# Second batch's fills and sums of squares rearranged, and three late output tiles stored by halves, in a fused cosine attention and GELU feed-forward kernel

## The chip, the cores and the metric

The kernel runs on one core of one Trainium2 chip. The metric is the device time of one execution in microseconds (us); the time of a kernel is the median of several runs.

## The reference

The input is q, k and v of shape 8 x 12 x 448 x 64 (batch, heads, sequence, head dimension), fp32, and two weight matrices. What is computed, cut to what matters:

```python
q_n = q / (norm(q, axis=-1) + 1e-6);  k_n = k / (norm(k, axis=-1) + 1e-6)
attn = softmax(q_n @ k_n.T / tau)                      # tau = 0.1
x = (attn @ v).transpose(0, 2, 1, 3).reshape(3584, 768)
h = x @ w_in                                           # 768 x 2048
out = (0.5 * h * (1 + erf(h / sqrt(2)))) @ w_out       # 2048 x 768, fp32 out
```

## The kernel before

The work of each of the 8 batches has three parts. *Attention* takes the 12 heads in three groups of four (`NQ = 3`); group g of the program is written g0 to g23 here, and the second batch (`b == 1`) has g3, g4 and g5. For a group, q and k are loaded (`load_qk`, the SP queue), squared on GpSimd (`square`, line 156), summed over the head dimension on VectorE (`reduce`, line 165), turned into inverse norms (ScalarE's logarithm and exponential, lines 172 to 192), multiplied in on GpSimd (`scale`, line 208) and turned by a DMA transpose on the SP queue (`transposes`, line 220). Then TensorE makes the scores in seven passes per group (`scores`, line 246), ScalarE the exponentials (`exps`, line 253), and `both` makes, in this order, the sums (`sums`, line 275), their turning and inversion on VectorE (lines 297 to 318), the values (line 289) and the normalised x (line 323). `first` is the product with w_in and the GELU (lines 649 and 685). `second_pieces` is the product with w_out for one token tile t and one column half ni: 16 matmuls (line 352), then a VectorE copy out of PSUM (line 356), and after the second half a store of the tile in two transfers of 64 rows each on the SP queue. `last_pieces` does the very last tile in three column parts.

The order is written out by hand (`manual_schedule`): each engine runs its instructions in the order in which the program issues them, and no scheduler moves any. The matmuls of `second_pieces` belong to the batches before and are kept as a list, `fill`. `attention(b, fill)` takes them out in six portions (`run`, sizes from `plan`), so that TensorE has work between the passes of scores (`visit`), each of which must wait for a pair of PSUM banks that `exps` frees. In the second batch the list holds 96 matmuls of six output tiles, numbered 1 to 6 here, 16 each. `upto(f, n)` calls `f` on all units below n that have not had it yet, so its place in the text is the place of that step in the engine's order. In `attention(1)` u is 4: units up to 8 are concerned, unit 7 is group g6 and unit 8 is group g7, both of the third batch.

Two PSUM banks (tags `mm0`, `mm1`) go round among the output tiles of `second_pieces`, with one buffer each; `sums` of a group takes the bank whose turn it is without passing the turn on. So a bank is free for its next user only when VectorE has copied or turned the content before.

All later batches have done `reduce` up to u+4 in `first`, before `attention` starts. Output buffers `ot` (pool `otp`) are three.

Of the kernel before, what the change touches and what calls it, by code (L numbers as in the profile page):

```python
# [16 lines left out]
def kernel(  # L17
# [17 lines left out]
    nc = tc.nc  # L35
    B, H, S, D = q.shape
# [7 lines left out]
    NH = d_model // 2  # L44
# [54 lines left out]
    def mm_tile(name, shape=(128, 512), dtype=F32, aside=None):  # L99
        t = ps_mm.tile(list(shape), dtype, tag=f"mm{turn[0] if aside is None else turn[0] ^ aside}", name=name)  # L100
        if aside is None:
            turn[0] ^= 1
        return t
# [65 lines left out]
    def logs(n):  # L169
        nq = nq_t.pop(n)  # L170
        ln_t[n] = nrm.tile(list(nq.shape), F32, tag="lq", name=f"lq{n}")
        nc.scalar.activation(ln_t[n], nq, AF.Ln, bias=tiny)

    def roots(n):
        ln = ln_t.pop(n)
        if n <= NQ:
            sr_t[n] = root2[n % len(root2)][:, :math.prod(shapes[n])]
            nc.scalar.activation(sr_t[n][:, :, 0], ln.rearrange("p j i s c -> p (j i s c)"), AF.Exp, scale=0.5)
        else:
            sr_t[n] = nrm.tile(list(ln.shape), F32, tag="sr", name=f"sr{n}")  # L180
            nc.scalar.activation(sr_t[n], ln, AF.Exp, scale=0.5)  # L181

    def inverses(n):
        sr = sr_t.pop(n)
        shape = [128] + shapes[n]
        se = nrm.tile(shape, F32, tag="se", name=f"se{n}")
        if n <= NQ:
            nc.vector.tensor_reduce(se.rearrange("p j i s c -> p (j i s c)"), sr, mybir.AxisListType.X, ALU.add)
        else:
            nc.gpsimd.tensor_scalar(se, sr, 1e-6, None, ALU.add)  # L190
        rn = nrm.tile(shape, F32, tag="rn", name=f"rn{n}")
        nc.vector.reciprocal(rn, se)  # L192
        rn_t[n] = rn
# [42 lines left out]
    def scores(g, banks, p=None):  # L236
        qkT = qkT_t[g]
        if p is None:
            p = st_turn[0]
            st_turn[0] ^= 1  # L240
        st = pair(p, f"st{g}_{banks[0][1]}")
        for n, (s, c) in enumerate(banks):
            rows = slice(64 * s, 64 * (s + 1))
            for h in range(2):
                cols = slice(64 * h, 64 * (h + 1))
                nc.tensor.matmul(st[cols, n, :S], lhsT=qkT[rows, 1, c, cols], rhs=qkT[rows, 0, :, cols],  # L246
                                 start=True, stop=True, tile_position=(64 * s, 64 * h))
        st_t[g, banks[0]] = st

    def exps(g, banks):  # L250
        st, m = st_t.pop((g, banks[0])), len(banks)
        pt = ptp.tile([128, 2, S], BF16, tag="pt", name=f"pt{g}_{banks[0][1]}")
        nc.scalar.activation(pt[:, :m], st[:, :m, :S], AF.Exp, scale=inv_tau)  # L253
        for n, (s, c) in enumerate(banks):
            pt_t[g, s, c] = pt[:, n]
# [69 lines left out]
    def both(g, p):  # L325
        sums(g)
        turned(g)
        inverted(g)
        spread(g, 0)
        spread(g, 1)  # L330
        values(g, p=p)
        normalise(g, 0)
        normalise(g, 1)
# [3 lines left out]
    def store(sb, t, src, c0, c1, engines):  # L337
        dst = out.rearrange("(b p c) d -> b c p d", b=B, c=C)
        for h in range(2):
            bb, c = divmod(2 * t + h, C)  # L340
            engines[h].dma_start(out=dst[2 * sb + bb, c, :, c0:c1], in_=src[64 * h:64 * (h + 1)])

    def second_pieces(sb, t, ni):
        state = {}

        def mm(kf):
            if kf == 0:
                state["ps"] = mm_tile(f"op{sb}_{t}_{ni}")
                if ni == 0:
                    ot_t[sb, t] = op_.tile([128, d_model], F32, tag="ot", name=f"ot{sb}_{t}")  # L350
            ps, ot = state["ps"], ot_t[sb, t]
            nc.tensor.matmul(ps[:, :NH], lhsT=g_t[sb][:, kf, t * 128:(t + 1) * 128],  # L352
                             rhs=wo[:, kf, ni * NH:(ni + 1) * NH],
                             start=(kf == 0), stop=(kf == KF - 1))
            if kf == KF - 1:
                nc.vector.tensor_copy(ot[:, ni * NH:(ni + 1) * NH], ps[:, :NH])  # L356
                if ni == 1:
                    store(sb, t, ot, 0, d_model, (nc.sync, nc.sync))

        return [lambda kf=kf: mm(kf) for kf in range(KF)]  # L360
# [33 lines left out]
    def upto(f, n, last=None):  # L394
        last = {load_qk: NG, load_v: NV, root: len(groups), load_wi: 4, load_wo: 4}.get(f, NU)
        while done.get(f, 0) < min(n, last):
            done[f] = done.get(f, 0) + 1
            f(done[f] - 1)
# [180 lines left out]
    def visit(b, pairs):  # L579
        for p in pairs:  # L580
            n, c = passes[at.get(b, 0)]
            at[b] = at.get(b, 0) + 1
            scores(b * NQ + n, ((0, c), (1, c)), p)
            exps(b * NQ + n, ((0, c), (1, c)))

    def attention(b, fill):
        fill = list(fill)
        plan = {96: (16, 14, 16, 18, 16, 16), 128: (20, 18, 20, 22, 32, 16)}[len(fill)]
        parts = iter(plan)

        def run():
            for _ in range(next(parts)):
                fill.pop(0)()

        x_t[b] = xp.tile([128, KD, S], BF16, tag="x", name=f"x{b}")
        g0, u = b * NQ, b * NQ + 1
        run()
        upto(scale, u + 3)
        upto(transposes, u + 3)
        if b == 1:  # L600
            upto(load_qk, g0 + NQ + 2)
            upto(square, u + 4)
        visit(b, (0, 1, 2))
        if b > 1:
            upto(scale, u + 4)
            upto(transposes, u + 4)
        run()
        visit(b, (0, 1, 2))
        run()
        upto(load_qk, g0 + NQ + 3)  # L610
        visit(b, (0, 1) if b <= 2 else (0, 1, 2))
        upto(square, u + 5)
        run()
        visit(b, (0, 1, 2))
        both(g0, 0)
        upto(load_v, b + 3)
        upto(load_qk, g0 + NQ + 4)
        visit(b, (1, 2))
        upto(reduce, u + 4 + (b > 1))
        run()  # L620
        visit(b, (1, 2, 0))
        both(g0 + 1, 1)
        visit(b, (2, 0))
        upto(reduce, u + 5)
        n = 2 * b + 4
        if n < len(groups):
            logs(n)
            roots(n)
        run()
        both(g0 + 2, 2)  # L630
        if n < len(groups):
            inverses(n)
            done[root] = n + 1
            if b > 1:
                visit(b + 1, (0, 1))
# [72 lines left out]
    fill = []  # L708
    for b in range(B):
        if b == 0:  # L710
            attention_first()
            acc.close()
            third.append(ctx.enter_context(tc.tile_pool(name="ps_third", bufs=1, space=bass.MemoryType.PSUM)))
        else:
            attention(b, fill)
        first(b)
        sb, hf = divmod(b, 2)
        todo = [(t, ni) for t in (range(3) if hf == 0 else range(3, 7)) for ni in range(2)]
        if b == 0:
            todo.sort(key=lambda x: x[1])  # L720
        tail = [2 * S // 128 - 1] if b == B - 1 else []
        fill = [f for t, ni in todo if t not in tail for f in second_pieces(sb, t, ni)]
        fill += [f for t in tail for f in last_pieces(sb, t)]
# [37 lines left out]
```

## Time and profile before

| | us |
|---|---|
| median of 5 runs (lowest, highest) | 416.92 (416.47, 418.09) |
| the profiled execution's own time | 418.31 |
| its span, first to last instruction | 416.5 |
| PE busy in the span | 406.1 (98%) |
| ScalarE busy | 246.3 (59%) |
| VectorE busy | 188.7 (45%) |
| GpSimd busy | 167.0 (40%) |
| granted TensorE clock, mean | 1.000 of full speed |

The profile records one execution. PE is the matmul part of TensorE, DVE is VectorE, ACT ScalarE, POOL GpSimd, SP the queue that issues most transfers. A row of the chain view has the start, the length and the work; a row of the timeline has start, length, engine, line, operation, tiles, shape and count, and in brackets how long the engine was idle before it and what ended that. Times in a row are us from the start of the span.

### The profile page before, as it was taken

The page shows a single profiled execution, that of the slowest core. Times are in us where ns is not written, and L with a number is a line of the kernel's source. Part 1 is how long each engine was busy: PE and PEld are TensorE (multiplying, and loading weights), DVE is VectorE, ACT ScalarE, POOL GpSimd, SP SyncE. Part 2 cuts the span into 40 slices and gives each one's busy share as a digit, 9 for nine tenths or more (in the row PEclk, how much of TensorE's full clock was granted, in tenths as well). Part 3 has the DMA queues.
Part 4 walks back from the last instruction along what each step waited for, and adds up shares of the span by engine and source line. Part 5 has one row for each costly group of instructions (what it writes and reads, how often), then busy time and mean ns, then how long its engine had stood idle before and what let it go on. Part 6 is the DMA issues. An engine that isn't in the chain of part 4 may idle for free.

```text
span 416.5 us, 8256 instructions
## 1 busy us (share of the span) xinstructions
PE 406.1 (98%) x3506; PEld 212.1 (51%) x3506; DVE 188.7 (45%) x379; ACT 246.3 (59%) x358; POOL 167.0 (40%) x113
## 2 busy tenths in 40 slices
PE   7899989899999999999999999999999999999996
PEld 3445545455555555555555555555545555555564
DVE  5787114933167322853148431683118711481021
ACT  5995686545755657745764548755655467754300
POOL 4999606066730719045540446318270243000000
PEclk9999999999999999999999999999999999999999
DMA  8999999635297314946297242975079120510033
GB/s 285 264 259 206 203 184 310 145 76 140 46 205 231 72 67 77 211 161 134 14 209 224 48 124 46 198 206 132 2 135 224 39 44 2 120 39 2 0 77 76
DMA packets 66516, 54.53 MB, mean 131 GB/s; under 512 B 38576, under 2 KB 61488, under 8 KB 66480
## 3 DMA queue, kind: packets, MB, share of 16 engines
q1 hardware_dynamic: 53984, 41.79, 39.2%
q0 software_dynamic: 12112, 11.80, 17.9%
q8 instruction: 27, 0.44, 0.4%
q10 hardware_dynamic: 384, 0.43, 0.3%
q14 instruction: 9, 0.07, 0.1%
HBM read 45.61 MB, written 11.01 MB: 136 GB/s over the span
## 4 chain that ended last, share of the span: by engine, by line
PE 81%; POOL 8%; DVE 4%; DMA 4%; issue 2%; ACT 0%; POOLq 0%
PE op L352 32%; PE hp L649 31%; PE st L246 7%; PE o L289 6%; POOL qkb L208 4%; PE sm L275 4%; DMA qkT<-qkb 3%; POOL sq L156 2%; DVE nq L165 2%; PE op L367 1%; POOL wi L381 1%; DMA qk<-in_q_dram 1%; DVE x L323 1%; POOL wo L388 0%; DVE tr L297 0%
## 5 line engine op out<-in xcount | busy, mean ns | idle before, releaser
L253 ACT ACTIVATE pt<-st 128x896 bf16<-128x896 f32 x168 | 142.9, 917 | 67.3 <-PE st L246 67.1
L649 PE MATMUL hp<-x,wi 128*128 128x448 bf16 x768 | 146.8, 353 | 1.2 <-DVE tr L297 1.2
L352 PE MATMUL op<-wo,g 128*128 128x384 bf16 x864 | 147.8, 326 | 0.0
L352 PEld LDWEIGHTS <-g 128*128 128x128 bf16 x864 | 81.5, 98 | 62.1 <-issue 10.7
L649 PEld LDWEIGHTS <-wi 128*128 128x128 bf16 x768 | 74.5, 98 | 72.5 <-issue 4.0
L685 ACT ACTIVATE g<-hp 128x448 bf16<-128x448 f32 x128 | 65.9, 545 | 68.3 <-PE hp L649 68.0
L208 POOL TENSOR_TENSOR qkb<-qk,rn 128x896 bf16<-128x896 f32 (+1 forms) x49 | 79.7, 1652 | 38.7 <-DVE rn L192 38.7
L356 DVE COPY ot<-op 128x384 f32<-128x384 f32 x54 | 29.6, 548 | 102.7 <-PE op L352 102.7
L165 DVE TENSOR_REDUCE nq<-sq 128x28 f32<-128x1792 f32 (+2 forms) x30 | 48.8, 1639 | 53.5 <-POOL sq L156 50.4
L156 POOL TENSOR_TENSOR sq<-qk 128x1792 f32<-128x1792 f32 (+1 forms) x22 | 66.5, 3037 | 15.2 <-DMA qk<-in_k_dram 15.2
L190 POOL TENSOR_SCALAR se<-sr 128x28 f32<-128x28 f32 (+1 forms) x14 | 4.4, 311 | 127.5 <-ACT sr L181 117.0
L246 PE MATMUL st<-qkT 64*64 64x448 bf16 x672 | 48.2, 358 | 2.5 <-DVE qkT L230 0.9
L289 PE MATMUL o<-pt,v 64*64 64x448 bf16 x672 | 36.9, 352 | 0.0
L246 PEld LDWEIGHTS <-qkT 64*64 64x64 bf16 x672 | 18.5, 105 | 26.6 <-issue 16.3
L318 DVE STREAM_TRANSPOSE rs<-rc 128x448 f32<-128x448 f32 x48 | 28.1, 623 | 0.8
L323 DVE TENSOR_TENSOR x<-o,rs 128x448 bf16<-128x448 f32 x48 | 27.0, 599 | 1.0 <-DVE rs L318 0.5
L289 PEld LDWEIGHTS <-v 64*64 64x64 bf16 x672 | 17.7, 106 | 16.9 <-issue 8.4
L192 DVE RECIPROCAL rn<-se 128x28 f32<-128x28 f32 (+2 forms) x18 | 6.8, 376 | 42.8 <-POOL se L190 42.6
L297 DVE STREAM_TRANSPOSE tr<-sm 128x448 f32<-128x448 f32 x24 | 15.5, 646 | 14.2 <-PE sm L275 11.1
L275 PE MATMUL sm<-pt,ones 128*32 128x448 bf16 (+1 forms) x336 | 17.8, 332 | 0.0
L309 DVE TENSOR_REDUCE tr<-tr 32x28 f32<-32x28 f32 x84 | 16.5, 196 | 1.6
L275 PEld LDWEIGHTS <-ones 128*32 128x32 bf16 x336 | 6.8, 95 | 9.0 <-issue 7.2
(43 smaller groups left out, 117.5 us busy)
## 6 DMA issues: line engine op xcount, KB each, us to landing
out_dram<-ot SPq DMA_DIRECT2D x54, 192.0 KB, 3.3
qk<-in_q_dram SPq DMA_DIRECT2D x23, 448.0 KB, 6.4
qk<-in_k_dram SPq DMA_DIRECT2D x23, 448.0 KB, 8.8
v<-in_v_dram POOLq DMA_DIRECT2D x7, 672.0 KB, 12.5
wi<-in_moe_w_in_dram POOLq DMA_DIRECT2D x8, 384.0 KB, 15.9
wo<-in_moe_w_out_dram POOLq DMA_DIRECT2D x4, 768.0 KB, 15.5
qk<-in_q_dram SPq DMA_DIRECT2D x2, 224.0 KB, 3.5
v<-in_v_dram POOLq DMA_DIRECT2D x1, 448.0 KB, 10.1
```

The source lines that it names most:

```text
L156: eng.tensor_tensor(sq[:, part], t[:, part], t[:, part], ALU.mult)
L165: nc.vector.tensor_reduce(nq[:, part], sq[:, part], mybir.AxisListType.X, ALU.add)
L208: eng.tensor_tensor(qkb[:, i, :, s0:s1].rearrange("p c s d -> p s c d"), t[:, i, s0:s1], rn[:, i].to_broadcast([128, s1 - s0, C, D]), ALU. ...
L246: nc.tensor.matmul(st[cols, n, :S], lhsT=qkT[rows, 1, c, cols], rhs=qkT[rows, 0, :, cols], start=True, stop=True, tile_position=(64 * s, 6 ...
L253: nc.scalar.activation(pt[:, :m], st[:, :m, :S], AF.Exp, scale=inv_tau)
L275: nc.tensor.matmul(bank_t[g, "sm"][r:r + 32, cols], lhsT=ones, rhs=pt_t[g, s, c][:, cols], start=(c < 2), stop=(c >= C - 2), tile_position ...
L289: nc.tensor.matmul(bank_t[g, h][cols, :S], lhsT=v_t[g][rows, s, c, :], rhs=pt_t[g, s, c][rows], start=(c == 0), stop=(c == C - 1), tile_po ...
L323: nc.vector.tensor_tensor(x_t[b][:, 2 * n + h, :], bank_t.pop((g, h))[:, :S], rs_t.pop((g, h)), ALU.mult)
L352: nc.tensor.matmul(ps[:, :NH], lhsT=g_t[sb][:, kf, t * 128:(t + 1) * 128], rhs=wo[:, kf, ni * NH:(ni + 1) * NH], start=(kf == 0), stop=(kf ...
L356: nc.vector.tensor_copy(ot[:, ni * NH:(ni + 1) * NH], ps[:, :NH])
L649: nc.tensor.matmul(hps[m], lhsT=wi[:, kd, m * 128:(m + 1) * 128], rhs=x_t[b][:, kd, :], start=(kd == 0), stop=(kd == KD - 1))
L685: nc.scalar.activation(g_t[sb][:, m, hf * S:(hf + 1) * S], hps.pop(m), AF.Gelu)
```

## The change

In the second batch the six portions of fill become 20, 13, 14, 17, 16, 16 matmuls in place of 16, 14, 16, 18, 16, 16 (96 in both). The sum of squares of unit 7 (g6) is issued ahead of the fourth portion of fill, where it was issued ahead of the fifth; the one of unit 8 (g7) is issued where g6's was, ahead of the fifth portion, and no longer behind `both` of the second group. For the other batches both calls of `reduce` find the same work as before. Of the last pair of batches (`sb == 3`), tiles 3, 4 and 5 are stored by column halves: after each copy two transfers of 64 rows x 384 columns, four per tile where there were two, on the SP queue.

```diff
             if kf == KF - 1:
                 nc.vector.tensor_copy(ot[:, ni * NH:(ni + 1) * NH], ps[:, :NH])
-                if ni == 1:
+                if sb == B // 2 - 1 and 3 <= t < 6:
+                    store(sb, t, ot[:, ni * NH:(ni + 1) * NH], ni * NH, (ni + 1) * NH, (nc.sync, nc.sync))
+                elif ni == 1:
                     store(sb, t, ot, 0, d_model, (nc.sync, nc.sync))
...
-        plan = {96: (16, 14, 16, 18, 16, 16), 128: (20, 18, 20, 22, 32, 16)}[len(fill)]
-        parts = iter(plan)
+        if len(fill) == 128:
+            parts = iter((20, 18, 20, 22, 32, 16))
+        else:
+            parts = iter((20, 13, 14, 17, 16, 16) if b == 1 else (16, 14, 16, 18, 16, 16))
...
         visit(b, (0, 1) if b <= 2 else (0, 1, 2))
+        upto(reduce, u + 4)
         upto(square, u + 5)
         run()
...
         visit(b, (1, 2))
-        upto(reduce, u + 4 + (b > 1))
+        upto(reduce, u + 5)
         run()
         visit(b, (1, 2, 0))
         both(g0 + 1, 1)
         visit(b, (2, 0))
-        upto(reduce, u + 5)
```

## The prediction

> **What bounds the kernel.** I read the page's busy shares first, then the waits of PE alone, then the chain of waits, then the timeline of the second batch and of the tail. Columns are as explained above.
>
> ```profile
> PE 406.1 (98%) x3506; PEld 212.1 (51%) x3506; DVE 188.7 (45%) x379; ACT 246.3 (59%) x358; POOL 167.0 (40%) x113
> ...
> out_dram<-ot SPq DMA_DIRECT2D x54, 192.0 KB, 3.3
> ```
>
> PE is busy for 406.1 us of the span's 416.5. The change neither adds nor removes a matmul, so all it can win or lose lies in the 10.4 us in which PE is idle. Asked by window, PE's waits show none at all from 104 to 388 us; in the second batch's attention (60 to 104 us) they are:
>
> ```profile
> PE hp L649 <- DVE tr L297: 1.2, 1, 1.2
> PE st L246 <- DMA qkT<-qkb: 0.9, 1, 0.9
> ```
>
> Total, times, longest. The first is the wait that ends the attention, the second a wait in the middle for g4's transpose. The chain says which work stands behind them:
>
> ```profile
> 47.29 13.44 DMA qkT<-qkb
> 60.77 0.57 PE st L246 x8
> ...
> 73.47 1.92 DVE nq L165
> 75.40 0.47 DVE ot L356
> 75.86 0.57 DVE tr L297
> ...
> 80.12 1.92 DVE nq L165
> 82.05 0.47 DVE ot L356
> 82.51 0.57 DVE tr L297
> 83.12 18.32 PE hp L649 x96
> ```
>
> g4's transpose, issued at 47.29, releases PE at 60.77. At the end VectorE stands on the chain: g7's sum of squares (80.12) delays the sixth tile's copy and g5's turning, and PE begins `first` at 83.12. The timeline gives the exact places:
>
> ```profile
> 56.78 0.38 PE L246 MATMUL st<-qkT 64*64 64x448 bf16 x4 [0.43 <-ACT pt L253]
> 63.29 3.17 POOL L156 TENSOR_TENSOR sq<-qk 128x1792 f32<-128x1792 f32 x1 [12.73 <-DMA qk<-in_k_dram]
> 65.02 0.56 DVE L356 COPY ot<-op 128x384 f32<-128x384 f32 x1 [2.65 <-PE op L352]
> 68.21 0.85 PE L275 MATMUL sm<-pt,ones 128*32 128x448 bf16 x16
> 81.88 0.10 PEld L649 LDWEIGHTS <-wi 128*128 128x128 bf16 x1 [0.36 <-issue]
> ```
>
> The 0.43 is a wait for a score bank that ScalarE frees. The second row is the one to keep in mind: g6's squares start when k of g6 lands and end at 66.46. The 65.02 row is tile 3's copy, the 68.21 row g3's sums, the last shows PE ready for `first` at 81.88, 1.24 us before it can start.
>
> **Fill.** One fill matmul takes 0.169 us in the chain (16 in 2.71), 12 score matmuls 0.69. Before, PE comes from 52.93 to the second portion at 57.10: 4.17 us for 2.71 + 0.69 of work, so 0.77 us are lost to ScalarE's banks. With 20 in the first portion the scores start at 52.93 + 20 x 0.169 = 56.32; the third pair is wanted at 56.78, when its bank is free, and the second portion starts at 57.01. So nearly the whole 0.77 is filled. With 13 more PE reaches g4's scores at 57.01 + 2.20 + 0.23 = 59.44 and waits for the same 60.77: 1.33 us in place of 0.91. At 60.77 it has 33 fill matmuls behind it and not 30. That is 3 x 0.169 = 0.51 us in hand; the portions of 14 and 17 keep it, and PE would reach g3's sums at 67.70 instead of 68.21.
>
> **The sum of squares of g6, moved up.** It now stands on VectorE ahead of tile 3's copy (tile 3 ends with the 48th fill matmul, and 47 are issued before). Behind it are the copies of tiles 3 and 4 and g3's turning. It cannot start before g6's squares end, 66.46; an earlier sum starts 0.03 us after its squares (40.16 to 40.19), so 66.49. From a sum's start to the end of the copy behind it takes 2.46 us (73.40 to 75.86), so tile 3 is out of its bank at 68.95. g3's sums take that very bank: it is tile 3's bank whose turn it is. With 0.05 us from VectorE to PE (82.43 + 0.64 to 83.12), the sums start at 69.00. A new wait of 1.30 us takes the place of PE's lead, and the sums are 0.79 us later than before. Tile 4 is not held up: its bank was copied out after the second tile.
>
> Also behind the late copy of tile 4 (68.2 to 69.4) is its store on the SP queue, and behind that the load of g9; both move by 1.3 us, and g9's squares are wanted only at 97, so the cover is over 20 us.
>
> **The sum of g7, moved up.** At its old place it costs PE the 1.24 us before 83.12. At its new one it starts after g3's x, at 73.40 + 0.79 = 74.19; its squares were done at 72.08, so it doesn't wait, and it does to the fifth copy and to g4's turning just what g6's did before. The first to feel it is tile 6's first matmul, which needs g4's turning (77.3) at 76.95 + 0.79 = 77.74: 0.4 us of cover, as before. From g3's sums to PE's readiness for `first` are 13.67 us (68.21 to 81.88), so 69.00 + 13.67 = 82.67. g4's x ends at 80.12 + 0.79 = 80.91, the sixth copy at 81.38, g5's turning at 82.02, before PE wants the bank. `first` starts at 82.67 to 82.72, not at 83.12: **0.40 to 0.45 us won**. From there PE is without idle time, so the gain reaches the end.
>
> A rule speaks against this order. The Trainium skill's page "SBUF — State Buffer" (on the shared port pair) says that GpSimd and a VectorE operation in a two-port mode lock each other out for a whole instruction. g7's squares on GpSimd (68.91 to 72.08) would then hold tile 4's copy for 3.17 us, and the kernel would be some 2.7 us slower. The row weighs more: the copy at 65.02 ran inside g6's squares and took 0.56 us, as did the one at 67.62 outside them. I take nothing for it.
>
> **The stores.** Six transfers more, each about 0.5 us of SP's issue time (the six old ones took 466 to 588 ns). SP is otherwise idle there: it waits for VectorE's copies before each tile's stores.
>
> ```profile
> 410.69 2.84 SPq L341 DMA_DIRECT2D out_dram<-last  x3
> 410.69 3.01 ACTq L341 DMA_DIRECT2D out_dram<-last  x3
> 412.74 0.29 DVE L370 COPY last<-op 128x128 f32<-128x128 f32 x1 [0.47 <-PE op L367]
> ```
>
> The end is set by PE's last part, its copy at 412.74, two small transfers that land 1.8 and 2.0 us after issue, and the closing waits. Tile 5's old stores, issued at 408.06 and 408.6, land 2.7 us later, at 411.3; the last copy wants their buffer at 412.74. So nothing on the path waits for a store, now or then: 1.4 us of cover. The page "DMA: Bandwidth & Descriptors" advises batches of at least 1 MiB and gives about 2 us fixed cost for each transfer. Paid one by one, six more would be 12 us; here 192 KB land in 2.7 us and overlap, and none is waited for. Bounds: a gain of 0.1 us if the last small transfers find emptier engines, a loss of 0.1 if the extra waits of the last copies show (17 ns each, two more for each of three copies). I take 0.
>
> **The sum.** 0.45 of a span of 416.5. The profiled execution took 418.31, 1.39 more than the median, and PE's work is fixed, so part of that is probably idle time for transfers that the other runs have less of. Against the median, with a little for that: 416.92 - 0.5 = **416.4**.
>
> **Rivals.** *Earlier transfers.* If g4's transpose lands over 0.9 us earlier in ordinary runs, PE before waits no longer there, and the fill's 0.77 is won in full; with g6's landing moving along (both follow each other on one queue, 60.77 and 63.29), at 1.4 us earlier the sums start at 67.3 before and 67.6 after: 1.24 - 0.3 = 0.95 won. With no wait at all in VectorE's way the most is 0.77 + 1.24 = 2.0: 414.9 to 416.0. For it: the profiled run is the slowest of the six shown. Against it: nothing in the trace shows which idle time shrank.
>
> *g6 lands later: slower.* The place is VectorE ahead of tile 3's copy; each us that k of g6 lands later than 63.29, with the transpose where it is, costs a full us, where before there were 6.9 us to spare (66.46 to 73.40). It decides from 63.7 on (gain gone), and from 64.5 on the loss exceeds 0.2%; at 65 it is 1.3 us: 418.2. For it: that load took 10.1 us to land, when the median of the ten such loads from 40 to 100 us is 5.4. Against it: it is right behind the transpose on the same queue, so the distance should be steady.
>
> *It does nothing.* The lead from the fill is lost to the new wait, and what g7's move wins is lost to the sums' delay: 416.8 to 417.0. This takes 0.4 us more delay than I count.
>
> **How the numbers follow.** Chances: the forecast 0.45 (its own range 415.9 to 416.7; a fifth of it past 0.2%), earlier transfers 0.33 (nearly all past it), later g6 0.14, nothing 0.08. A difference below 0.2%, or 0.83 us, is about what a measurement of this kernel can't tell from no change. Faster: 0.09 + 0.33 = 0.42; slower: 0.13; same: 0.45. The range from 415.3 to 417.3 leaves out the far end of the earlier transfers and most of the slower case, under 2 in 10.
>
> **What would show it.** Right: PE's wait of 1.2 us for VectorE ahead of `first` is gone; one of about 1.3 us ahead of g3's sums (line 275 before the change) is new, ended by tile 3's copy; the wait for g4's transpose grows to about 1.3; the 0.43 wait for ScalarE is gone; the last copy is not waiting for a store. Wrong: sums of g3 that start without a wait (the gain is then larger), g6's squares ending after 67 (smaller), or a tail past the last copy that differs from 3.4 us by over 0.2.

## The result and the profile after

The changed kernel takes 415.63 us (median of 27 runs, 415.22 to 419.51) and the kernel before, with more runs, 416.74 (47 runs). The ratio is 0.9977 with a 95% interval of 0.9966 to 0.9988: 0.96 us faster, between 0.5 and 1.4. The profiled execution took 416.43, with a span of 414.6.

The page of the changed kernel, engine totals and two groups (line, engine, operation, tiles and shape, count, busy time, mean, idle time ahead and what ended it); line 655 is the old 649:

```profile
PE 406.1 (98%) x3506; PEld 212.1 (51%) x3506; DVE 188.6 (45%) x379; ACT 246.1 (59%) x358; POOL 166.9 (40%) x113
...
L655 PE MATMUL hp<-x,wi 128*128 128x448 bf16 x768 | 146.8, 353 | 0.0
...
L275 PE MATMUL sm<-pt,ones 128*32 128x448 bf16 (+1 forms) x336 | 17.8, 332 | 1.3 <-DVE ot L356 1.3
```

PE's busy time is what it was, 406.1 us. The idle time ahead of `first` (1.2 us before) is 0.0, and 1.3 us ahead of the sums, ended by a copy, are new. The chain of waits shows who ends it (start, length, work):

```profile
51.80 10.18 DMA qk<-in_k_dram
...
62.10 3.18 POOL sq L156
...
65.31 2.02 DVE nq L165
67.33 0.48 DVE ot L356
...
67.85 0.85 PE sm L275 x16
```

The load of g6, its squares on GpSimd, its sum and tile 3's copy on VectorE now stand on the chain in a row, up to g3's sums. From there PE works through to the end, where the old chain ran over VectorE almost without a break from 69.1 to 83.1 us. The timeline has the same places, and the copy that begins the tail:

```profile
59.57 0.57 PE L246 MATMUL st<-qkT 64*64 64x448 bf16 x8 [0.55 <-DMA qkT<-qkb]
67.25 1.01 DVE L356 COPY ot<-op 128x384 f32<-128x384 f32 x2
67.58 3.17 POOL L156 TENSOR_TENSOR sq<-qk 128x1792 f32<-128x1792 f32 x1 [2.30 <-DMA qk<-in_k_dram]
67.85 0.85 PE L275 MATMUL sm<-pt,ones 128*32 128x448 bf16 x16 [1.26 <-DVE ot L356]
81.49 18.33 PE L655 MATMUL hp<-x,wi 128*128 128x448 bf16 x96
411.13 0.29 DVE L374 COPY last<-op 128x128 f32<-128x128 f32 x1 [0.47 <-PE op L371]
```

Tiles 3 and 4 are copied in one go after g6's sum, and the sums wait 1.26 us for the first of the two copies. The squares at 67.58 are g7's.

Absolute times shift with the start of each execution, so I count from the second batch's first fill matmul (52.93 before, 52.25 after). Before, `first` starts 83.12 - 52.93 = 30.19 us after it, after the change 81.49 - 52.25 = 29.24: 0.95 less. The two executions are not alike, though: g6's squares, which wait for a load, start 63.29 - 52.93 = 10.36 us after that matmul before and 62.10 - 52.25 = 9.85 after, so 0.51 of the 0.95 came with an earlier load. From the last copy's start to the end of the span it is 416.46 - 412.74 = 3.72 before and 414.62 - 411.13 = 3.49 after: 0.23 less. The rest of the 1.8 us between the two spans (0.68) lies ahead of the second batch, where the change does nothing.

### The profile page after: what moved, and what is told of

Read it like the earlier page. It is cut to its first block, busy times and chain, and to the rows that moved or that the text cites. A ratio compares the mean times of both kernels' runs of the same rounds, so it can differ in the third digit from the quotient of the medians.

```text
span 414.6 us, 8268 instructions
## 1 busy us (share of the span) xinstructions
PE 406.1 (98%) x3506; PEld 212.1 (51%) x3506; DVE 188.6 (45%) x379; ACT 246.1 (59%) x358; POOL 166.9 (40%) x113
## 4 chain that ended last, share of the span: by engine, by line
PE 87%; POOL 4%; DMA 3%; DVE 2%; ACT 1%; issue 1%; SPq 0%; POOLq 0%; DVEq 0%
PE op L352 32%; PE hp L655 31%; PE st L246 9%; PE o L289 8%; PE sm L275 4%; POOL qkb L208 3%; DMA qk<-in_k_dram 2%; POOL sq L156 2%; DVE nq L165 2%; PE op L371 1%; PE sm L266 1%; DMA qk<-in_q_dram 1%; PE tp L225 1%; PE spin L407 0%; ACT pt L253 0%
```

## The experiments

Three things were open: whether the early sum of g6 costs PE what the forecast says, why the gain is about twice the forecast, and what shortened the tail.

### Each part alone

Fill alone:

```diff
-        plan = {96: (16, 14, 16, 18, 16, 16), 128: (20, 18, 20, 22, 32, 16)}[len(fill)]
+        plan = {96: (20, 13, 14, 17, 16, 16) if b == 1 else (16, 14, 16, 18, 16, 16), 128: (20, 18, 20, 22, 32, 16)}[len(fill)]
```

> Only the fill of the second batch (20, 13, 14, 17, 16, 16); sums of squares and stores as before. My account (each part's effect is not additive, because the early sum of g6 makes PE wait): with g6's sum left at its old place the 3 fill matmuls in hand at g4's transpose (0.51 us) go through to the end, and the 1.2 us wait ahead of first stays: 0.5 to 0.8 us faster than before. Rival (fill's lead is worth nothing, all of the measured gain of 0.96 us comes from the sum of g7): within 0.2 us of before.

Measured: ratio 0.9987 (0.9977 to 0.9998), 0.5 us faster. PE's waits of this kernel from 60 to 104 us are one line:

```profile
PE hp L649 <- DVE tr L297: 1.2, 1, 1.2
```

The old wait ahead of `first` stands as it was, and the one for ScalarE's bank is gone. g4's transpose was late here too, though no wait is listed for it:

```profile
58.49 1.07 PE L246 MATMUL st<-qkT 64*64 64x448 bf16 x12
```

Such a pass of 12 takes 0.76 us where nothing holds it; here the records have the transpose landing 6.84 us after the first fill matmul and the first scores that need it starting at 6.88, some 0.3 us late.

Sums of squares alone:

```diff
         visit(b, (0, 1) if b <= 2 else (0, 1, 2))
+        upto(reduce, u + 4)
         upto(square, u + 5)
...
-        upto(reduce, u + 4 + (b > 1))
+        upto(reduce, u + 5)
...
-        upto(reduce, u + 5)
         n = 2 * b + 4
```

> Only the two sums of squares moved; fill (16, 14, 16, 18, 16, 16) and stores as before. My account: g3's sums wait for tile 3's copy behind g6's sum, at the same time as with the whole change, since that time is set by g6's load and not by PE; the wait is about 0.8 us instead of 1.3 and the 1.2 us wait ahead of first is gone: as fast as the whole change within 0.2 us, 0.4 to 1.0 us faster than before. Rival (the parts add up): slower than the whole change by 0.5 us or more.

Measured: ratio 0.9977 (0.9964 to 0.999), the ratio of the whole change. PE's waits from 45 to 104 us, in total:

```profile
PE st L246 <- ACT pt L253: 0.4, 1, 0.4
PE sm L275 <- DVE ot L356: 0.8, 1, 0.8
```

0.8 us ahead of the sums instead of 1.3, as expected: the sums start when the copy allows it, and the fill only changes how long PE waits for that. So by the profiles fill and sums are not additive; the times (0.5 and 1.0 us for the parts, 1.0 for the whole, each to about half a us) could not tell alone.

Stores alone:

```diff
-                if ni == 1:
+                if sb == B // 2 - 1 and 3 <= t < 6:
+                    store(sb, t, ot[:, ni * NH:(ni + 1) * NH], ni * NH, (ni + 1) * NH, (nc.sync, nc.sync))
+                elif ni == 1:
```

> Only tiles 3, 4 and 5 of the last pair of batches stored by halves. My account: nothing waits for a store, so within 0.1 us of before. Rival (the tail past the last copy, 3.7 us before and 3.5 us with the whole change in the two profiles, is shortened by the halves): 0.2 to 0.3 us faster than before, and a tail of 3.5 us in its profile. Second rival (fixed cost for each transfer shows): slower by 0.5 us or more.

Measured: ratio 0.999 (0.9974 to 1.0006), an interval too wide for 0.2 us, but the profile has a tail (from the last copy's start to the end of the span) of 415.24 - 411.73 = 3.51. My "nothing" falls by the profile. A loss of 0.5 us or more, the second rival, lies outside the interval.

### What shortens the tail

The same halves on other tiles, six transfers more but none near the end:

```diff
-                if sb == B // 2 - 1 and 3 <= t < 6:
+                if sb == B // 2 - 1 and t < 3:
```

> The kernel before, with the halves on tiles 0, 1 and 2 of the last pair of batches: six transfers more, some 20 us and more ahead of the end, and the last tiles stored whole as before. Theory (the number of transfers decides: the semaphores of the SP and ACT transfers go round by eight, the program's closing waits run through them in order, and six transfers more put the last two on the seventh and eighth, so that no closing wait is left behind the last landing): the time from the last copy's start to the end of the span is 3.5 us, as with the whole change, not 3.7. Rival (smaller last stores leave the DMA engines emptier): 3.7 us.

Measured: tail 415.51 - 412.00 = 3.51, with the last tiles stored whole. So it is not that the last stores are small. This is one execution, of 417.28 us (the kernel before, median of 7 beside it: 416.56); only its tail is used.

Eight more:

```diff
-                if sb == B // 2 - 1 and t < 3:
+                if sb == B // 2 - 1 and 2 <= t < 6:
```

> The kernel before, with the halves on tiles 2, 3, 4 and 5 of the last pair of batches: eight transfers more. Theory (count of transfers by eight): the last two land on the same semaphores as before, so from the last copy's start to the end of the span 3.7 us. Rival (smaller last stores): 3.5 us.

Measured: tail 415.26 - 411.07 = 4.19, which neither foresaw; one execution again, of 417.06 us. The closing waits of SP (total, times, longest) separate the parts; they are of the kernel before, the whole change, the six early transfers and the eight, in this order:

```profile
SPq L756 <- DMA out_dram<-last: 1.5, 1, 1.5
```

```profile
SPq L762 <- DMA out_dram<-last: 1.1, 2, 0.7
```

```profile
SPq L758 <- DMA out_dram<-last: 1.2, 2, 0.7
```

```profile
SPq L758 <- DMA out_dram<-last: 1.5, 1, 1.5
```

With eight more, SP waits once and for 1.5 us as before; with six more, twice. In SP's records the wait that the last landing ends is over 2.38 us after the last copy's start in all four. In the kernel before and with eight more, seven closing waits still follow it, 0.06 us apart, to 2.81 and 2.84. With six more a single one follows, at 2.48. The records also show why: the semaphores of the SP and ACT transfers go round by eight, and the closing waits go through the eight in a fixed order. The last two transfers have the first and second of them in the kernel before and with eight more, the seventh and eighth with six more. So the number of transfers sets how many closing waits stand behind the last landing: 0.33 us of SP's time, of which 0.2 reach the end. All profiles agree on the size: five with the stores as before have tails of 3.69 to 3.72, seven with six more transfers 3.49 to 3.51. With eight more the last wait comes as before, and some 0.45 us are then added in the drains and semaphores behind it. Why stays open.

### The kernel before once more

> The kernel before, unchanged, for a second profile. Theory (the late landing of g4's transpose was that one execution's): no wait for the transpose ahead of g4's scores, and PE starts first 29.1 us after the first fill matmul of the second batch, not 30.2. Rival (it is the usual course): a wait of about 0.9 us and 30.2 us.

Measured: the transpose was late again, 0.8 us of waiting, and `first` 30.06 us after the first fill matmul. My theory that the late landing was one execution's falls. But four other kernels keep the second batch as before, and there it varies. All profiles but that of the double squares in the changed kernel, which follows below, counted from the second batch's first fill matmul, in us:

| kernel | g6's squares start | g3's sums | `first` | `first` minus squares |
|---|---|---|---|---|
| before | 10.36 | 15.28 | 30.19 | 19.83 |
| before, again | 10.25 | 15.16 | 30.06 | 19.81 |
| six early transfers | 9.96 | 14.88 | 29.80 | 19.84 |
| eight transfers | 9.48 | 14.39 | 29.31 | 19.83 |
| squares twice, before | 9.10 | 14.17 | 29.08 | 19.98 |
| stores alone | 8.03 | 14.17 | 29.08 | 21.05 |
| fill alone | 9.43 | 13.83 | 28.75 | 19.32 |
| whole change | 9.85 | 15.60 | 29.24 | 19.39 |
| sums alone | 9.27 | 15.01 | 28.65 | 19.38 |
| copy first | 8.75 | 13.52 | 27.20 | 18.45 |
| copy first, again | 8.62 | 13.52 | 27.20 | 18.58 |
| copy first, more fill | 8.88 | 13.52 | 27.19 | 18.31 |

The squares start when k of g6 lands, right behind g4's transpose on one queue. With fill and sums as before, `first` comes 19.81 to 19.84 us after their start when transfers are late, and never earlier than 29.08 us after the first fill matmul; the two rows with 29.08 have no wait for a transfer, so that is what the old order takes with early ones. With the early sums it is 19.39 and 19.38, with and without the new fill, and both profiles have the wait for tile 3's copy. So the gain is 0.44 us where transfers are late, and more where they are early: with a landing at 9.1 it would be 29.08 - 9.1 - 19.39 = 0.6, at 8.6 it would be 1.1. That is worked out from the rows' differences, not measured pair by pair. With the fill alone, whose transpose was late, `first` comes 19.32 us after the squares' start: with late transfers each part alone wins about what the whole wins. With earlier ones the fill's gain should end near 0.65 us (14.17 to 13.52, the start of g3's sums where nothing is late), since it leaves the wait ahead of `first`; no profile shows that. The edits are not what moves the landing: the whole change and copy first are one program up to the third portion of fill, and g4's transpose, which lands ahead of that portion, comes at 7.28 and 6.17 in the records.

### The suspected wait made longer

g6's squares computed twice over, into the same tile with the same values, in the changed kernel and in the one before:

```diff
-                eng.tensor_tensor(sq[:, part], t[:, part], t[:, part], ALU.mult)
+                for _ in range(2 if u == 7 else 1):
+                    eng.tensor_tensor(sq[:, part], t[:, part], t[:, part], ALU.mult)
```

> The whole change, with g6's squares computed twice over on GpSimd (3.17 us more ahead of g6's sum, same values). Theory (g6's sum holds tile 3's copy, whose bank g3's sums take): the wait ahead of g3's sums grows from 1.3 to 4.4 us, and the kernel is 3.1 to 3.3 us slower than the whole change, 2.0 to 2.3 slower than before. Rival (the copy is not what PE waits for, or the cover is elsewhere): less than 1 us slower than the whole change.

> The kernel before, with g6's squares computed twice over on GpSimd (3.17 us more, same values). Theory: g6's sum is wanted at its old place only 6.9 us after its squares end, so the whole 3.17 us are covered: within 0.2 us of before, where the same addition cost the whole change 4.9 us (3.1 by the wait, the rest by half the TensorE clock after it). Rival (GpSimd's load itself costs, by g7's squares starting 0.7 us later or by contention with VectorE): slower by 0.7 us or more.

Measured: with the change 1.0083 (1.006 to 1.0106), 3.5 us slower than before and 4.4 slower than the whole change by the ratios (4.9 by the medians); without it 1.0002 (0.9989 to 1.0015). The same 3.17 us on GpSimd are free in the old order, to within the interval of 0.6 us, and cost more than themselves in the new. The timeline and windows of the changed kernel with the double squares, whose line numbers are one higher (windows: stretch, length, busy time of PE, PEld, DVE, ACT and POOL, granted clock, DMA share, GB/s):

```profile
70.88 1.50 PE L276 MATMUL sm<-pt,ones 128*32 128x448 bf16 x16 [4.50 <-DVE ot L357]
```

```profile
66.00:70.80 4.80, 0.39 (x11) 0.09 (x1) 2.45 (x3) 2.54 (x3) 4.80 (x2) 0.91 0.63 227
70.80:76.70 5.90, 5.82 (x55) 2.39 (x55) 4.59 (x13) 1.14 (x2) 1.49 (x2) 0.50 0.65 120
76.70:82.00 5.30, 5.30 (x74) 2.73 (x73) 3.94 (x8) 3.12 (x4) 0.00 (x0) 0.99 1.14 287
```

The wait grew to 4.50 us, as foreseen (4.4). After it the granted clock is 0.50 for 5.9 us of work; the same 16 sums take 1.50 us instead of 0.85. From g6's squares to `first` it is 25.41 us instead of 19.39: 6.0 more, 3.17 for the squares and some 2.9 for half the clock. This is the slowest of the four executions, with a mean granted clock of 0.992; the other three have 0.995 or 0.996 and so lost less to the clock, which fits the smaller 4.4 to 4.9 us between the times.

### The wait taken away

One fill matmul moved from the fourth portion to the third, so that tile 3 ends in the third portion and its copy is ahead of g6's sum:

```diff
-            parts = iter((20, 13, 14, 17, 16, 16) if b == 1 else (16, 14, 16, 18, 16, 16))
+            parts = iter((20, 13, 15, 16, 16, 16) if b == 1 else (16, 14, 16, 18, 16, 16))
```

> The whole change, but the second batch's fill is 20, 13, 15, 16, 16, 16: the third portion ends tile 3, so its copy is ahead of g6's sum on VectorE and g3's sums find their bank free. Mechanism of the forecast (the sum of g6 holds that copy, and PE waits 1.3 us for it): the wait of 1.3 us ahead of g3's sums is gone and first starts 1.2 us earlier than with the whole change: 2.0 to 2.3 us faster than before. Rival (another wait close behind takes its place, g3's turning or x late behind g6's sum and tile 4's copy): under 0.5 us faster than the whole change.

> copy_first once more beside copy_first_more. Theory: 2.0 to 2.3 us faster than before, as in its first run. Rival (its first run was a lucky chip): 1 us or less.

Measured: 0.9948 (0.9932 to 0.9964), and in the second run 0.9952 (0.9936 to 0.9967): 2.2 and 2.0 us faster than before, by the ratios 1.2 and 1.0 faster than the whole change. Its timeline:

```profile
62.46 0.56 DVE L356 COPY ot<-op 128x384 f32<-128x384 f32 x1 [2.84 <-PE op L352]
64.68 2.02 DVE L165 TENSOR_REDUCE nq<-sq 128x28 f32<-128x1792 f32 x1 [1.67 <-POOL sq L156]
66.25 0.85 PE L275 MATMUL sm<-pt,ones 128*32 128x448 bf16 x16
66.62 0.55 DVE L356 COPY ot<-op 128x384 f32<-128x384 f32 x1
```

The copy at 62.46 is ahead of the sum at 64.68, and the sums at 66.25 start without a wait. Tile 4's copy is still behind the sum, but g3's turning, the next in line, is wanted only by the fifth portion, and PE has no wait of VectorE left from 45 to 110 us. This version beats both kernels. All its profiles had early transfers.

Four more matmuls ahead of g4's scores:

```diff
-            parts = iter((20, 13, 15, 16, 16, 16) if b == 1 else (16, 14, 16, 18, 16, 16))
+            parts = iter((20, 17, 11, 16, 16, 16) if b == 1 else (16, 14, 16, 18, 16, 16))
```

> As copy_first, but the fill is 20, 17, 11, 16, 16, 16: four matmuls from the third portion to the second, ahead of g4's scores, whose transpose lands late in some executions. Theory (after copy_first only that wait of 0 to 0.9 us is left in the second batch): 0 to 0.6 us faster than copy_first, 2.2 to 2.8 us faster than before. Rival (with PE earlier, g6's sum and tile 4's copy hold g3's turning and x, and a new wait ahead of the fifth portion appears): as fast as copy_first or slower.

Measured: 0.9943 (0.9926 to 0.996) beside 0.9952 for copy_first on the same chip, medians 414.59 and 415.07. The intervals overlap, and in the profiles `first` comes at 27.19 and 27.20. Whether it helps when the transpose is late stays open, since it was late in neither.

## Why the prediction was right, and where it was off

*The early sum of g6.* Right, and to 0.05 us: forecast, a wait of 1.30 us ended by tile 3's copy, measured 1.26; forecast, `first` 82.67 - 63.29 = 19.38 us after g6's landing, measured 19.39 and, with the sums alone, 19.38. The experiment with the copy ahead shows the mechanism by taking it away, the double squares by stretching it. No sign of a smaller gain came: g6's squares end at 65.27 in the profile after, not after 67.

*The sum of g7.* Right: the 1.2 us ahead of `first` is gone, with the sums alone too.

*The fill.* The lead was there, a little smaller than "nearly the whole 0.77": where nothing is late, g3's sums come 13.52 us after the first fill matmul with the new first portion and 14.17 with the old, 0.65 less. In the whole change it is worth little: the fill alone wins 0.5 us, the sums alone as much as everything together. The forecast said that the new wait takes the lead's place.

*The transfers' state.* Here the size was off. I took the profiled execution's late transposes (wait of 0.91) as the usual case, with a chance of 0.45, and said that the wait would grow to 1.3; in the profile after it was 0.55. Of the thirteen profiles, five show a wait for the transpose (0.91, 0.80, 0.55, 0.51 and 0.44 us), two more are held up by 0.2 to 0.3 us without one being listed (eight transfers, fill alone), and six are not held up. So the rival of earlier transfers holds for a good part of the executions. It was a little too large: for a landing 1.4 us earlier it said 0.95 won, the table's rows give 29.08 - 8.96 - 19.39 = 0.73. What share of the timed runs has which state no run shows.

*The stores.* The step "I take 0" failed. I looked for a transfer that something waits for, found none, and did not look at the closing waits themselves, which lie on the path. Their term is 0.2 us in the profiles. Counted from the last copy's end, as the forecast did, the tail went from 3.43 to 3.20 us, which is just over the difference of 0.2 that it had named as a sign of being wrong. That no store is waited for was right: the first of the last tile's three copies starts 2.64 us ahead of the last one in both profiles.

*The sum.* 0.44 to some 1.1 in the second batch, by the transfers' state, and 0.2 in the tail: 0.6 to 1.3, measured 0.96, forecast 0.5. The direction was right. The time lies in the range, and 0.3 below the forecast's own narrower one: the range held because it had been drawn wide enough for the rival of earlier transfers, and the tail's 0.2 stood in neither.

*The slower rival.* Its mechanism is real: 3.17 us more ahead of g6's sum lengthened the wait from 1.26 to 4.50. No profile had so late a load. "Each us later costs a full us" is too little at that wait, where the clock fell too; where between 1.26 and 4.50 us that begins no run shows.

*The rules weighed.* g7's squares, from 67.58 on, did not hold tile 4's copy: the two copies from 67.25 on took 1.01 us. Whether this copy, out of PSUM, is one that the rule speaks of no trace here shows. The price of about 2 us for each further transfer did not appear either (stores alone, ratio 0.999).

## What to carry to other kernels

When work is moved up on an in-order engine, look at the bank that the instruction right behind it frees and who takes that bank next: one fill matmul more ahead of it was worth 1.0 to 1.2 us here, as much as the whole change. Read a wait for a transfer from several profiles before counting on it, and give the gain for both cases. The end of a program has waits of its own, and how many of them stand behind the last landing can depend on how many transfers came before.

## What the runs showed of the hardware

A wait of 4.50 us brought TensorE's granted clock to 0.50 for 6.8 us. That is worked out from the rows of the double squares: a mean of 0.91 over 4.80 us is 0.50 for the last 0.86 of them, then come 5.90 at 0.50 and less than 0.1 in the last row. So the clock fell at 69.9, some 3.5 us after PE's last matmul had ended at 70.88 - 4.50 = 66.38. The wait of 1.26 us in the profile after left it at 1.00. The Trainium skill, "TensorE: Matmul & The Clock Gate" (Part 1), gives about 3.4 us of idle time for the fall, which agrees. And each closing wait on SP takes 0.06 us even when what it waits for is long done (the seven from 2.44 to 2.81 us after the last copy's start in the kernel before).
